# A list scheduler's model of three engines, and the order that it writes for a two-layer transformer kernel

## The chip, the cores and the metric

The kernel runs on one core of a Trainium2 chip. The core has five instruction streams that run side by side and meet at semaphores: TensorE (PE, matrix products), ScalarE (ACT, activation functions), VectorE (DVE, elementwise work), GpSimd (POOL) and SyncE (SP, which issues the transfers). Each of them works through its own list in order. The metric is the device time of one execution in microseconds (us).

## The reference

Two layers are computed one after the other, with the same weights in both: attention with 32 heads of 16 columns, then a dense block with GELU. There are 2048 rows of 512 columns, in bf16.

```python
def _A_ref(x, wqkv, wo):                       # S = 2048, D = 512, H = 32, Dh = 16
    qkv = (x @ wqkv).reshape(B, S, 3, H, Dh).transpose(2, 0, 3, 1, 4)
    q, k, v = qkv[0], qkv[1], qkv[2]
    scores = einsum("bhqd,bhkd->bhqk", q, k) * (Dh ** -0.5)
    p = softmax(scores, axis=-1)
    o = einsum("bhqk,bhkd->bhqd", p, v)
    return o.transpose(0, 2, 1, 3).reshape(B, S, D) @ wo

def _B_ref(x, w1, b1, w2, b2):                 # F = 1792
    h = gelu(einsum("bsd,df->bsf", x, w1) + b1)
    return einsum("bsf,fd->bsd", h, w2) + b2

x = x + _A_ref(layernorm(x), wqkv, wo); x = x + _B_ref(layernorm(x), w1, b1, w2, b2)
x = x + _A_ref(layernorm(x), wqkv, wo); x = x + _B_ref(layernorm(x), w1, b1, w2, b2)
```

## The kernel before

**Cells.** The scores are cut into cells of 128 keys x 512 columns, where the 512 columns are the queries of one head, or of two heads in segments of 256. There are 4,096 cells in the two layers. A pass is one segment of queries and one group of heads; it has four row groups (a = 0 to 3) and 16 key tiles, or a part of them.

**Two ways to an exponential.** TensorE computes the score of a cell into a bank of PSUM (L1137). Most cells go to ScalarE, which takes two or three banks in one instruction (L1466) and writes the probabilities into `pt`. Others go to VectorE: an eviction (`dfirst`, L1283) turns a score into the bits of a bf16 number by a multiply and an add in uint16. Then `dchain` adds a shift to those bits in two further instructions (L1344, L1346), so that four shifted patterns stand in `du`. Each pattern is multiplied with V scaled by a weight of its own (`vc`, copied by GpSimd at L1068), and TensorE sums the four in PSUM. A cell on VectorE therefore asks TensorE for four products with V, one on ScalarE for one. `dchain` works on pairs of cells where it can, or on a single. A column `du`, `dh`, `kt` in the profile's groups names the buffer that holds the patterns. The table `KD` allows VectorE four key tiles of 16 in each layer. What VectorE has not taken when a pass runs out of other cells goes to ScalarE (`next_act`).

**Banks.** PSUM has eight. Banks 0 to 2 and 3 and 4 are two slots (`SLOTS`) that ScalarE empties in turn, bank 5 (`PVB`) gathers the products with V, and banks 6 and 7 serve projections and VectorE's cells.

**The order is written by a simulation.** A generator for each piece of work yields operations (`_Op`) with an engine, a cost in us, and what they read and write. `_Sched.run` keeps a clock for each engine and takes the operation that can start first; among those that could start now on one engine the priority decides. It writes the operations into each engine's list in that order, with the semaphore waits that they need. On the chip the lists run as they stand, so the modelled times have a say only in the order, and in what is decided from the modelled state. These things are decided from it:

- An operation's result is there at its end plus `LATENCY` of its engine (L205, L390). `_cost` (L301) gives the time for which the engine is taken; `SW` = 0.107 is added where TensorE changes between kinds of products.
- A score product may be late by its `slack`, which is the larger of `SLACK` (0.3 us) and the modelled length of the exponential in the other slot less `LATE` (0.7 us). Other TensorE work is taken first only if it ends within that.
- `attach` (L1215) adds up to two VectorE cells to a score operation, if bank 6 or 7 is free within `TOL` = 0.2 us of its start, a `du` buffer is to be had and little other VectorE work waits. `swap` (L1192) turns the third cell of a ScalarE slot into a VectorE cell, if VectorE's modelled clock is no more than `SWAP` = 0.5 us ahead of the start. `solo` places a VectorE cell by itself where ScalarE's modelled clock is far ahead of TensorE's.
- `fill` (L312) puts products without a use into TensorE's modelled gaps, so that it is not idle for long. `free` (L1090) chooses the bank for them. A product into bank 5 has weights of zero and adds nothing to the sum that is gathered there (L1125, `ps<-vc,zero`).

The costs in the code that the change works on are 0.68 us for `dfirst`, 0.08 + 0.14n and 0.08 + 0.28n for the two steps of `dchain` with n cells, 0.065 + 0.4267n for an exponential of n cells, and `MM` = 0.2132 us for a round of four products.

Of the kernel before, what the change touches and what calls it, by code (L numbers as in the profile page):

```python
# [201 lines left out]
        self.done = False  # L202


LATENCY = {"pe": 0.20, "act": 0.103149, "dve": 0.099491, "pool": 0.153328, "sp": 0.1}  # L205


class _Sched:
# [90 lines left out]
        return max(self.end.get(self.P.lastw[k], 0.0) if k in self.P.lastw else 1e9 for k in keys)  # L299

    def _cost(self, op):  # L301
        return op.cost + (SW if op.eng == "pe" and op.mode != self.mode else 0.0)

    def active(self, t):
        while self.stream and self.stream[0][1] < t - WINDOW:
# [6 lines left out]
    def fill(self, start, nxt):  # L312
        while self.filler and self.mode:
# [17 lines left out]
            self.clock["pe"] = now + into + MM + cold  # L331
            self.end[ev] = self.clock["pe"] + LATENCY["pe"]

    def run(self):
        while True:
# [53 lines left out]
            self.clock[e] = start + cost  # L389
            self.end[ev] = start + cost + op.tail + LATENCY[e]  # L390


SW = 0.107
# [108 lines left out]
class _Plan:  # L502
# [587 lines left out]
    def free(self, now, ahead):  # L1090
        P = self.P
        best = (None, 1e9)
        src = self.source()
        for b in (6, 7, 0, 1, 2, 3, 4, 5) if src else ():
            k = "B.%d" % b
            if k in ahead or b in self.hold or k in P.lastw and not P.reads.get(k) and P.lastw[k] not in self.s.fills:
                continue
            t = max([0.0] + [self.s.end.get(ev, 0.0) + FOLD for ev in P.deps(src, [k]) if ev[0] != "pe"])
            if max(t, now) < max(best[1], now):
                best = (b, t)  # L1100
        k = "B.%d" % PVB
        if best[1] > now and self.pvopen and "VC.0.0" in P.lastw and k not in ahead:
            best = (PVB, 0.0)
        return best
# [65 lines left out]
    def take(self, c, free):  # L1170
        self.scored += 1
        self.left[c[0]] -= 1
        if self.left[c[0]] == 0:
            free.append(self.s.tokens[("qp", c[0])])

    def join(self, op, d, b, extra, free):
        pools = self.s.pools
        if self.open is None:
            self.open = {"du": pools["du"].pop(0), "cells": [], "full": False}
        pair = self.open  # L1180
        pair["cells"].append(d)
        extra.append((d, b, pair, len(pair["cells"]) - 1))
        if len(pair["cells"]) == self.cap[pair["du"]]:
            self.open = None
        f, r = self.score(d, self.s.tokens[("qp", d[0])], b)
        op.fns.append(f)
        op.reads += r
        op.writes.append("B.%d" % b)
        self.take(d, free)
        self.nd += 1  # L1190
# [431 lines left out]
```

## Time and profile before

| what | value |
|---|---|
| median of three runs | 1588.72 us (1586.61, 1589.74, 1588.72) |
| span of the profiled execution, first to last instruction | 1584.3 us |
| the profiled execution's own total | not recorded; the median lies 4.4 us above its span |
| busy: TensorE, VectorE, ScalarE | 1432.2, 1355.7, 1545.8 us |
| score products (L1137) | 4,096 |
| VectorE evictions of scores (L1283) | 716 + 92 + 81 = 889 |
| mean granted TensorE clock | 0.998 |
| share of the time in which the DMA engines moved data (q1) | 21.2% |

A group's line gives the line of the kernel, the engine, the operation, output and input by the program's names with their shapes, the count, then busy time and mean duration of one, then the idle time before them and what ended it. A recorded duration goes from an instruction's start to its end; where the next one starts before that end, the engine's time for one is shorter than the duration, and busy time counts an overlap once. The chain that ended last is followed back from the last instruction through what released each one.

### The profile page before, as it was taken

How to read it: one execution, taken by the hardware profiler on the slowest of the kernel's cores; microseconds unless marked ns; L12 is line 12 of the kernel's file. 1: busy time of each engine (PE TensorE's matmuls, PEld its weight loads, DVE VectorE, ACT ScalarE, POOL GpSimd, SP SyncE). 2: the span in 40 equal slices, each digit the busy share in tenths (PEclk: the TensorE clock that was granted, in tenths of full speed). 3: DMA queues.
4: the chain of work that ended last, by engine and by line, in shares of the span. 5: the costliest groups of instructions: out<-in, count | busy, mean ns of one | idle time of the engine just before them, and what ended most of it. 6: DMA issues, size and time to landing. Idle time of an engine off the chain costs nothing.

```text
span 1584.3 us, 43090 instructions
## 1 busy us (share of the span) xinstructions
PE 1432.2 (90%) x18795; PEld 447.9 (28%) x18795; DVE 1355.7 (86%) x2558; ACT 1545.8 (98%) x1392; POOL 200.9 (13%) x250
## 2 busy tenths in 40 slices
PE   8998889999999898998989989888898889889988
PEld 3222222222222222322222222222222222333344
DVE  5689999779998889989799789999789978988894
ACT  7999999999999999999999999999999999999995
POOL 5200011010110201002110020122002000010000
PEclk9999999999999999999999999999999999999999
DMA  5100001341014211152111521001251006213420
GB/s 141 22 1 2 1 16 34 95 126 43 22 48 135 80 41 28 42 149 66 35 28 48 159 50 35 1 14 28 84 151 43 26 9 174 82 36 101 142 82 29
DMA packets 141768, 96.90 MB, mean 61 GB/s; under 512 B 36877, under 2 KB 141582, under 8 KB 141582
## 3 DMA queue, kind: packets, MB, share of 16 engines
q1 hardware_dynamic: 141582, 94.14, 21.2%
q8 instruction: 150, 2.46, 0.6%
q14 instruction: 36, 0.29, 0.1%
HBM read 84.41 MB, written 2.10 MB: 55 GB/s over the span
## 4 chain that ended last, share of the span: by engine, by line
ACT 65%; PE 30%; DVE 2%; POOL 1%; DMA 1%; issue 1%; SPq 0%; POOLq 0%; ACTq 0%
ACT pt L1466 58%; PE ps L512 12%; PE ps L1137 9%; PE ps L1527 9%; ACT g L893 2%; ACT v L1466 1%; ACT kt L1466 1%; ACT q L1466 1%; DVE du L1283 1%; ACT L893 1%; PE ps L1125 1%; DMA xf<-xln 1%; DVE du L1346 0%; ACT L1466 0%; DVE du L1344 0%
## 5 line engine op out<-in xcount | busy, mean ns | idle before, releaser
L1466 ACT ACTIVATE pt<-ps 128x1536 bf16<-128x1536 f32 (+1 forms) x1264 | 1387.1, 1259 | 10.5 <-PE ps L1137 6.4
L1137 PE MATMUL ps<-qp,kt 32*128 32x512 bf16 x4096 | 534.7, 384 | 129.9 <-ACT pt L1466 91.5
L1283 DVE TENSOR_SCALAR du<-ps 128x512 uint16<-128x512 f32 x716 | 484.5, 686 | 92.7 <-PE ps L1137 85.9
L1527 PE MATMUL ps<-pt,v 128*17 128x512 bf16 (+1 forms) x3386 | 444.9, 359 | 3.2 <-DVE v L739 1.1
L1137 PEld LDWEIGHTS ps<-qp,kt 32*128 32x128 bf16 x4096 | 141.2, 91 | 677.1 <-ACT pt L1466 286.1
L1527 PE MATMUL ps<-du,vc 128*17 128x512 bf16 (+1 forms) x2403 | 326.6, 359 | 1.3 <-DVE du L1344 0.6
L1346 DVE TENSOR_SCALAR du<-du 128x2048 uint16<-128x2048 uint16 (+1 forms) x361 | 246.7, 686 | 2.2
L1085 POOL TENSOR_SCALAR qp<-q,mask 128x512 bf16<-128x512 bf16 (+1 forms) x91 | 66.9, 735 | 1005.5 <-PE ps L1137 996.4
L512 PE MATMUL ps<-xf,wr 128*32 128x512 bf16 (+1 forms) x2400 | 171.2, 369 | 3.0 <-DMA xf<-xln 1.6
L1344 DVE TENSOR_SCALAR du<-du 128x1024 uint16<-128x1024 uint16 (+1 forms) x361 | 152.6, 433 | 2.2
L1527 PE MATMUL ps<-du,v 128*17 128x512 bf16 (+1 forms) x801 | 148.3, 360 | 0.8 <-DVE du L1346 0.5
L1527 PEld LDWEIGHTS ps<-pt,v 128*17 128x17 bf16 x3386 | 114.4, 88 | 114.8 <-issue 76.6
L512 PE MATMUL ps<-wr,g 128*32 128x512 bf16 x1600 | 123.2, 386 | 3.9 <-ACT g L893 3.2
L1527 PEld LDWEIGHTS ps<-du,vc 128*17 128x17 bf16 x2403 | 91.0, 89 | 65.4 <-issue 30.2
L872 DVE TENSOR_SCALAR g<-ps,hb1t 128x512 bf16<-128x512 f32 (+1 forms) x112 | 79.9, 713 | 15.3 <-PE ps L512 13.9
L1527 PE MATMUL ps<-dh,vc 128*17 128x512 bf16 (+1 forms) x309 | 86.4, 357 | 0.0
L1283 DVE TENSOR_SCALAR dh<-ps 128x512 uint16<-128x512 f32 x92 | 63.0, 685 | 9.3 <-PE ps L1137 7.9
L512 PEld LDWEIGHTS ps<-xf,wr 128*32 128x32 bf16 x2400 | 52.5, 95 | 61.9 <-issue 33.6
L1283 DVE TENSOR_SCALAR kt<-ps 128x512 uint16<-128x512 f32 x81 | 55.5, 685 | 14.9 <-PE ps L1137 13.9
L602 POOL TENSOR_SCALAR xln<-x,rstd,nmr 128x512 bf16<-128x512 bf16 x58 | 56.3, 973 | 30.9 <-DMA xf<-xln 21.6
L1125 PE MATMUL ps<-vc 128*32 128x512 bf16 x520 | 54.7, 384 | 0.0
L754 POOL TENSOR_TENSOR ott<-xt,rc 128x256 bf16<-128x256 f32 x42 | 33.3, 792 | 164.3 <-DVE rc L746 158.8
(93 smaller groups left out, 1184.5 us busy)
## 6 DMA issues: line engine op xcount, KB each, us to landing
wr<-in_B_w_dram SPq DMA_DIRECT2D x256, 256.0 KB, 2.8
wr<-in_A_wqkv_dram SPq DMA_DIRECT2D x24, 256.0 KB, 2.9
wr<-in_A_wo_dram SPq DMA_DIRECT2D x18, 256.0 KB, 2.9
out_dram<-x SPq DMA_DIRECT2D x16, 128.0 KB, 2.6
g<-in_A_wqkv_dram SPq DMA_DIRECT2D x3, 512.0 KB, 6.0
x<-in_A_x_dram SPq DMA_DIRECT2D x3, 512.0 KB, 8.8
q<-in_B_w_dram SPq DMA_DIRECT2D x3, 512.0 KB, 5.5
kt<-in_B_w_dram SPq DMA_DIRECT2D x4, 256.0 KB, 3.3
```

Of the source, the lines that this page charges most:

```text
L512: return [lambda e, a=a: e.matmul(out[32 * a:32 * a + 32, :], lhsT=lhsT[:, 32 * a:32 * a + 32], rhs=rhs, start=start, stop=stop, tile_posi ...
L602: yield _Op(eng, cost, lambda e: e.tensor_scalar(T["XLN"][:, x, :], T["X"][:, t, :], T["RSTD"][:, t:t + 1], T["NMR"][:, t:t + 1], op0=ALU. ...
L872: yield _Op("dve", 0.21 + n / 966, lambda e, fc=fc, pb=pb: e.tensor_scalar(T["G"][:, fc, q], pb, T["HB1T"][:, fc:fc + 1], None, op0=ALU.ad ...
L893: lambda e, g=g: e.activation(out=g, in_=g, func=ACT.Gelu_apprx_tanh), reads=gk, writes=gk, prio=2)
L1085: yield _Op("pool", 0.1 + 0.6 * w / 512, lambda e, s=s, q=q, i=i, t=t, w=w: e.tensor_scalar(T["QP"][:, s, w * i:w * i + w], q, T["MASK"][: ...
L1125: fns.append(lambda e, o=o, w=w, a=a, m=m: e.matmul(o, lhsT=w, rhs=rhs, start=start, stop=start, tile_position=(0, m * a)))
L1137: return (lambda e: e.matmul(o, lhsT=lhsT, rhs=rhs, start=True, stop=True, tile_position=(32 * a, 0)), ["K%d.%d.%d" % (l, gb, kt // 4), "Q ...
L1283: yield _Op("dve", 0.68, lambda e: e.tensor_scalar(u, self.bank(b), E_SCALE, E_BIAS, op0=ALU.mult, op1=ALU.add), reads=["B.%d" % b], write ...
L1344: yield _Op("dve", 0.08 + 0.14 * n, lambda e: e.tensor_scalar(U[:, 1, 0:n, :], U[:, 0, 0:n, :], SHIFT, None, op0=ALU.add), reads=key[0], w ...
L1346: yield _Op("dve", 0.08 + 0.28 * n, lambda e: e.tensor_scalar(U[:, 2:4, 0:n, :], U[:, 0:2, 0:n, :], 2 * SHIFT, None, op0=ALU.add), reads=k ...
L1466: yield _Op("act", 0.065 + 0.4267 * n, lambda e, src=src, dst=dst: e.activation(out=dst, in_=src, func=ACT.Exp, scale=0.25), reads=["B.%d" ...
L1527: op.fns.append(lambda e, o=o, lhsT=q[0][0][m], rhs=q[0][1][:, n * m:n * m + n], a=a, st=st, sp=sp: e.matmul(o, lhsT=lhsT, rhs=rhs, start= ...
```

## The change

The latencies of TensorE, ScalarE and VectorE in the model are raised. A VectorE operation takes its engine for 0.083 us less than its cost, and for no less than 0.07 us. A TensorE operation of kind "P" (products with V, projections) takes 2% longer. And bank 5 is no longer in the list from which `free` takes a filler's bank first; it is still taken when no other is free and its sum is open. No operation's own code is changed: which cells go to which engine, and the order in every list, follow from the simulation run anew.

```diff
-LATENCY = {"pe": 0.20, "act": 0.103149, "dve": 0.099491, "pool": 0.153328, "sp": 0.1}
+LATENCY = {"pe": 0.219, "act": 0.21, "dve": 0.139, "pool": 0.153328, "sp": 0.1}
+OVERLAP = 0.083
+ROUND = 1.02
...
     def _cost(self, op):
-        return op.cost + (SW if op.eng == "pe" and op.mode != self.mode else 0.0)
+        if op.eng == "dve":
+            return max(op.cost - OVERLAP, 0.07)
+        if op.eng == "pe":
+            return op.cost * (ROUND if op.mode == "P" else 1.0) + (SW if op.mode != self.mode else 0.0)
+        return op.cost
...
-        for b in (6, 7, 0, 1, 2, 3, 4, 5) if src else ():
+        for b in (6, 7, 0, 1, 2, 3, 4) if src else ():
```

## The prediction

> **What bounds the kernel now.** I read the page's busy shares first, then the chain that ended last, then the groups kept apart by shape, the table of waits, and at last one short stretch in order of time. The first view asks which engine has no room:
>
> ```profile
> PE 1432.2 (90%) x18795; PEld 447.9 (28%) x18795; DVE 1355.7 (86%) x2558; ACT 1545.8 (98%) x1392; POOL 200.9 (13%) x250
> ACT 65%; PE 30%; DVE 2%; POOL 1%; DMA 1%; issue 1%; SPq 0%; POOLq 0%; ACTq 0%
> ```
>
> ScalarE (ACT) is full, and the chain runs through it or through TensorE (PE) for 95% of the span. VectorE (DVE) is on it for 2%, so a faster VectorE helps only by taking work from ScalarE. The stretches say where room is:
>
> ```profile
> 0.00:100.00 100.00, 95.30 (x1186) 29.43 (x1186) 64.25 (x132) 90.41 (x92) 33.56 (x55) 1.00 0.25 65
> 100.00:200.00 100.00, 82.83 (x940) 22.65 (x938) 93.45 (x178) 99.74 (x90) 9.73 (x12) 1.00 0.01 2
> 300.00:400.00 100.00, 92.84 (x1167) 27.29 (x1169) 82.10 (x151) 99.63 (x91) 10.16 (x12) 1.00 0.34 96
> 700.00:800.00 100.00, 92.04 (x1138) 26.01 (x1138) 82.54 (x154) 99.75 (x95) 17.32 (x20) 1.00 0.22 62
> ```
>
> The columns are length, then busy PE, weight load, DVE, ACT, POOL with counts. In the three later ones ScalarE is above 99%, while VectorE stands idle for 6 us of 100 in the first stretch after the opening and for 18 in the others shown.
>
> Now the times that the scheduler's model is compared with, by group (count, then busy us, mean ns of one, idle before):
>
> ```profile
> L1466 ACT ACTIVATE pt<-ps 128x1024 bf16<-128x1024 f32 x771 | 806.9, 1092 | 3.0 <-PE ps L1137 2.1
> L1466 ACT ACTIVATE pt<-ps 128x1536 bf16<-128x1536 f32 x493 | 750.0, 1521 | 7.4 <-PE ps L1137 4.3 <-PE ps L1527 1.5
> L1283 DVE TENSOR_SCALAR du<-ps 128x512 uint16<-128x512 f32 x716 | 484.5, 686 | 92.7 <-PE ps L1137 85.9
> L1344 DVE TENSOR_SCALAR du<-du 128x1024 uint16<-128x1024 uint16 x355 | 151.2, 436 | 2.2
> L1346 DVE TENSOR_SCALAR du<-du 128x2048 uint16<-128x2048 uint16 x355 | 244.3, 691 | 2.2
> ```
>
> The table of waits (us in total, times, longest) has the two that matter between the engines:
>
> ```profile
> PE ps L1137 <- ACT pt L1466: 91.5, 239, 1.0
> DVE du L1283 <- PE ps L1137: 85.9, 188, 2.9
> ```
>
> And the stretch in order of time, VectorE's lines alone:
>
> ```profile
> 801.37 0.28 DVE L1344 TENSOR_SCALAR dh<-dh 128x512 uint16<-128x512 uint16 x1
> 801.57 0.42 DVE L1344 TENSOR_SCALAR du<-du 128x1024 uint16<-128x1024 uint16 x1
> 801.91 0.42 DVE L1346 TENSOR_SCALAR dh<-dh 128x1024 uint16<-128x1024 uint16 x1
> 802.24 1.10 DVE L1346 TENSOR_SCALAR du<-du 128x2048 uint16<-128x2048 uint16 x1
> ```
>
> In the last fence the columns are start and duration: each instruction starts 0.08 to 0.09 us before the one ahead of it has ended. Over the whole trace 1,717 of 2,558 VectorE instructions start so.
>
> **The constants against these rows.** For an exponential of three cells the old model has its result at 0.065 + 3 x 0.4267 + 0.103 = 1.448 us after its start; the row says 1.521. For two cells it is 1.021 against 1.092. With 0.21 it becomes 1.555 and 1.128, 0.034 to 0.036 behind the recorded ends. That explains the first wait shown: the old order puts a score product 0.07 us too early behind an exponential, and TensorE, which works in order, stands for 91.5 us. For VectorE the old model takes 0.68 for an eviction (L1283); the trace starts the next one 0.60 later, and 0.68 - 0.083 = 0.597. TensorE's 0.213 + 0.219 = 0.432 lies behind a recorded 0.384.
>
> One family is over-corrected. The two shift-and-add steps of a pair cost 0.36 and 0.64 in the code, so 0.277 and 0.557 in the new model; in the fence the first takes 0.34 to its successor, and back to back the second takes 0.60. Singles become 0.137 and 0.277 against 0.20 and 0.33. With 394 pairs and 101 singles (groups L1344, L1346) the new model is short by 394 x (0.063 + 0.043) + 101 x (0.063 + 0.056) = 54 us of VectorE time, where the old one was long by about 25.
>
> A page of the Trainium skill speaks against the overlap: "VectorE: DVE Perf Modes", section "The DRAIN you can't avoid", has the next Vector instruction wait until the pipe of the one before is empty. By that rule alone the sum would hold no extra cells, and 2,558 x 0.083 = 212 us of planned VectorE time would be missing on the chip. The last fence and the count above it show the opposite for two thirds of the instructions, and the measurement decides.
>
> **The change, part by part.** (1) VectorE's planned time falls by at most 2,558 x 0.083 = 212 us. What uses it are `swap` and `attach`, which hand a score cell to VectorE when its planned queue, a bank and a pattern buffer are free soon enough. VectorE now takes 716 + 92 + 81 = 889 of 4,096 cells (the L1283 groups); the code allows 4 of 16 key tiles, 1,024. Of the 135 missing, about 33 belong to the first 100 us, where 17 of 200 cells went to VectorE because the scaled copies of V come late; 102 are in reach. In 100 to 200 us it took 72 of 290, the full quarter, with 6.5 us idle, so the quarter can be carried where little else lies on it. In 300 to 400 us and 700 to 800 us it took 56, with 18 us idle. A cell costs 0.60 + (0.34 + 0.60)/2 = 1.07 us. The thirteen stretches of 100 us from 200 to 1500 are 87.8% busy on the mean; brought to the 93.45% of the full one they give 13 x 5.65 = 73 us, or 69 cells. Ends: 20 cells if banks and buffers hold as now, 100 if all in reach move. I take 60, a little under the 69, since a bank must be free at the right moment too. On ScalarE a cell is worth 1521 - 1092 = 429 ns: 60 x 0.429 = 25.7 us off a path that ScalarE sets. 20 cells give 8.6, 100 give 42.9.
>
> (2) Each moved cell asks for four column products instead of one. Four make a round of about 0.22 us (rounds start 0.22 apart at L1527), so 0.16 us of TensorE a cell, 10 us for 60. TensorE carries 30% of the chain: 3 us are charged, 0 to 10 the bounds. The rest lies in the 91.5 us of waits at L1137.
>
> (3) The 54 us that VectorE's chains are planned short: VectorE's 228 us of idle time cover most. Without that cover a late VectorE instruction keeps a bank, a score product waits for it, and behind it on TensorE all P·V rounds and projections. Bounds 0 and 54; a fifth of the span (100 to 300 and 1000 to 1100 us) is over 93% busy and has little cover, so I take 54 x 300/1584 = 10.
>
> (4) Later ScalarE and TensorE results move score products back by about 0.1 us in the order and put P·V rounds where TensorE waited. By start-to-start times, what follows a two-cell exponential comes 37 us late in total over its 0.903 us, 28 of these in 82 gaps of over 0.2 us that stand behind P·V or projection work. A truer plan can win back some 20; but the allowance of 0.3 us for a late score is unchanged, and with 0.21 + 0.107 + 0.213 + 0.219 = 0.749 of 0.918 us used, a score at its limit leaves ScalarE 0.13 us short. Bounds -20 and +15; taken as 0.
>
> (5) TensorE's rounds 2% longer in the plan, bank 5 out of the list for fillers, other places for DMA issues on SP and for GpSimd's masks: 0. Fillers (1,048 products at L1125) go only where TensorE would stand; if the 528 into bank 5 went without replacement, the granted clock of 0.998 could fall, and 2% of TensorE's 30% of the chain would be 9 us. Weight loads land in 2.8 us with a DMA share of 0.2, far ahead of use. Opening and tail (the last 26 us have no exponential) can shift by 5 either way.
>
> Sum: the profiled span of 1584.3 - 25.7 + 3 + 10 + 0 = 1571.6; the median of the runs lies 4.4 above that span (the profiled execution's own total is not given), so **1576.0**. With the 13 us of costs in proportion to the cells, 20 cells give 1588.7 - 8.6 + 4.3 = 1584.4, and 100 cells give 1588.7 - 42.9 + 21.7 = 1567.5, or 1552 if 15 of the 20 us in (4) come too: this case's own range is 1552 to 1584.
>
> **Rivals.** A: the score ring runs late. Place: L1137 behind a two-cell exponential. There are 792 of them (x771 and the smaller groups); if half of the scores that follow sit at the 0.3 us limit, 396 x 0.13 = 51 us of gaps stand where 37 are now, and P·V work, now free to fill, makes one score in four later by another 0.1, 792/4 x 0.1 = 20 us. With 20 cells moved and their 4.3 of costs: 1588.7 + 34 - 8.6 + 4.3 = 1618 with all of it, 1601 with half. It decides once the gaps grow by more than the cells save, 8.6 us for 20 of them and 25.7 for 60. For it: 82 gaps exist already, and allowance and margins were left. Against: gaps over 0.2 us come of a plan that had results early, which is mended.
>
> B: VectorE becomes the pacing engine. If 40 of the 54 us reach the path, 1588.7 - 25.7 + 3 + 40 = 1606. It decides from 25.7 - 3 = 22.7 us. Against it: 14% idle VectorE.
>
> C: no more cells, since pattern buffers are freed by TensorE, not by VectorE. Then only (4) and noise in the order remain: 1588 +- 4. Against it: the 85.9 us in which L1283 waited for a score.
>
> **How the numbers follow.** A change of 0.2% (3.2 us) is about what can be told from none here. Forecast 0.56, of which 0.55 faster and 0.01 same; A 0.20 and B 0.12, of which 0.30 slower and 0.02 same; C 0.12, a third to each side. That makes faster 0.59, same 0.07, slower 0.34. The range takes the forecast's lower bound, 1552, and reaches up to B's 1606, past the middle of A; left out are the upper part of A and B, and below it more cells than 100 or all of the gaps.
>
> **What would show it.** Right: L1283 above 930 products, three- and two-cell exponentials holding fewer than 3,170 cells, VectorE's share up, the wait of L1137 for ScalarE well under 91.5 us. A: start-to-start excess behind two-cell exponentials above 50 us. B: L1137 waiting for L1283 above 40 us (10.1 now) with VectorE over 95% busy. C: L1283 within 15 of 889. A longer tail or a clock under 0.98 would be none of these, and the prediction wrong in its cause.

## The result, and the profile after

The changed kernel takes 1606.7 us (median of four runs, 1606.6 to 1608.9), the kernel before on the same chip 1587.9 us. The ratio is 1.0129, with a 95% interval of 1.0108 to 1.0150: slower by about 20 us where 1576 was forecast. The profiled span grew from 1584.3 to 1604.9 us.

Lines of before are shown above; these answer to them. Line numbers are 6 higher after the change (L1137 is L1143, L1283 is L1289, L1466 is L1472). First the busy shares and the chain that ended last, from the page of after:

```profile
PE 1427.3 (89%) x18923; PEld 438.2 (27%) x18923; DVE 1401.6 (87%) x2695; ACT 1532.4 (95%) x1389; POOL 204.7 (13%) x250
DVE 50%; PE 30%; ACT 18%; issue 1%; POOL 0%; DMA 0%; DVEq 0%
```

ScalarE has less to do and is a smaller share of a longer span. VectorE, 2% of the chain before, is half of it now, although its busy share rose by one point only. The share is an average; the stretches show where it is full (length, then busy PE, weight load, DVE, ACT, POOL, then the granted clock, the DMA share and GB/s). Three further stretches of before come first, then those of after:

```profile
200.00:300.00 100.00, 92.32 (x1083) 26.46 (x1080) 93.47 (x177) 98.30 (x90) 12.67 (x13) 1.00 0.11 30
1000.00:1100.00 100.00, 82.74 (x915) 23.21 (x911) 94.24 (x187) 98.24 (x88) 22.74 (x29) 1.00 0.05 12
1200.00:1300.00 100.00, 87.74 (x1073) 25.49 (x1075) 87.63 (x163) 99.76 (x85) 12.34 (x14) 1.00 0.10 25
```

```profile
100.00:200.00 100.00, 81.06 (x966) 21.87 (x956) 99.48 (x194) 96.29 (x87) 9.72 (x12) 1.00 0.01 2
200.00:300.00 100.00, 89.37 (x1088) 24.07 (x1084) 97.35 (x189) 95.83 (x89) 12.86 (x13) 1.00 0.12 30
300.00:400.00 100.00, 92.88 (x1191) 26.82 (x1194) 86.47 (x166) 98.48 (x91) 11.54 (x12) 1.00 0.33 94
1200.00:1300.00 100.00, 87.33 (x1090) 24.26 (x1084) 98.83 (x193) 94.89 (x88) 13.10 (x13) 1.00 0.11 28
```

From 100 to 300 and from 1200 to 1300 us VectorE has hardly any idle time left, and ScalarE, at 99.7% from 100 to 200 us before, is at 96.3%. The table of waits names the path from the one to the other (us in total, times, longest), two lines of before first:

```profile
PE ps L1137 <- DVE du L1283: 10.1, 18, 1.0
ACT pt L1466 <- PE ps L1137: 6.4, 14, 1.8
```

```profile
PEld ps L1143 <- DVE du L1289: 162.7, 288, 1.8
PE ps L1143 <- ACT pt L1472: 65.6, 155, 1.5
DVE du L1289 <- PE ps L1143: 61.2, 81, 4.7
ACT pt L1472 <- PE ps L1143: 37.7, 99, 1.4
PE ps L1143 <- DVE du L1289: 31.2, 73, 1.5
```

The first line of after is the weight loads that stand ahead of the score products; they wait for the same evictions. The score products themselves wait for VectorE's evictions (31.2 us, 10.1 before; with the buffers `dh` and `kt` 42.3, 14.1 before), and ScalarE waits for the score products: 37.7 us, 6.4 before. VectorE in its turn waits less for scores, 61.2 us for 85.9.

The groups kept apart by shape give the cells:

```profile
L1472 ACT ACTIVATE pt<-ps 128x1024 bf16<-128x1024 f32 x818 | 827.6, 1057 | 20.0 <-PE ps L1143 17.3
L1472 ACT ACTIVATE pt<-ps 128x1536 bf16<-128x1536 f32 x430 | 639.0, 1486 | 23.2 <-PE ps L1143 20.4
L1289 DVE TENSOR_SCALAR du<-ps 128x512 uint16<-128x512 f32 x763 | 510.0, 683 | 63.1 <-PE ps L1143 61.2
```

With the smaller groups VectorE evicts 763 + 100 + 87 = 950 cells, 61 more than before, and ScalarE's 844 exponentials of two cells and 486 of three hold 3,146.

**The books.** An exponential is followed by the next after 0.903 us (two cells) or 1.330 us (three) where nothing is late. What the start-to-start times hold above that I call gaps. Before: 37.1 us behind two cells and 3.7 behind three, 40.8 in all. After: 76.5 + 14.0 = 90.5. So gaps +49.7; 61 cells fewer at 1.330 - 0.903 = 0.427 us are -26.0; the tail behind the last exponential is 26.5 us for 29.2, -2.7. The sum is +21.0, the span grew by 20.6. The gain came as forecast, and the gaps took it twice over. The question is where 50 us of gaps come from. All gaps below are read in the same way, each from one profiled execution; executions of one kernel differ by some us (those of before from 1582.4 to 1591.9), so a difference of a few us between two gaps tells nothing.

### The profile page after: what moved, and what is told of

Same layout as the page of the kernel before. It is cut to its first block, busy times and chain, and to the rows that moved or that the text cites. A ratio compares the mean times of both kernels' runs of the same rounds, so it can differ in the third digit from the quotient of the medians.

```text
span 1604.9 us, 43512 instructions
## 1 busy us (share of the span) xinstructions
PE 1427.3 (89%) x18923; PEld 438.2 (27%) x18923; DVE 1401.6 (87%) x2695; ACT 1532.4 (95%) x1389; POOL 204.7 (13%) x250
## 4 chain that ended last, share of the span: by engine, by line
DVE 50%; PE 30%; ACT 18%; issue 1%; POOL 0%; DMA 0%; DVEq 0%
DVE du L1289 18%; ACT pt L1472 12%; PE ps L518 12%; PE ps L1143 9%; PE ps L1533 9%; DVE du L1352 8%; DVE du L1350 5%; ACT g L899 3%; DVE dh L1289 2%; DVE g L878 2%; DVE kt L1289 2%; DVE stats L587 2%; DVE dh L1352 1%; DVE xt L749 1%; DVE kt L1352 1%
## 5 line engine op out<-in xcount | busy, mean ns | idle before, releaser
L1472 ACT ACTIVATE pt<-ps 128x1024 bf16<-128x1024 f32 (+1 forms) x1248 | 1358.1, 1205 | 43.3 <-PE ps L1143 37.7
L1143 PE MATMUL ps<-qp,kt 32*128 32x512 bf16 x4096 | 531.6, 386 | 127.4 <-ACT pt L1472 65.6
L1289 DVE TENSOR_SCALAR du<-ps 128x512 uint16<-128x512 f32 x763 | 510.0, 683 | 63.1 <-PE ps L1143 61.2
L1533 PE MATMUL ps<-pt,v 128*17 128x512 bf16 (+1 forms) x3276 | 423.0, 361 | 6.3 <-DVE du L1352 2.4
L1143 PEld LDWEIGHTS ps<-qp,kt 32*128 32x128 bf16 x4096 | 138.3, 91 | 665.3 <-ACT pt L1472 217.9
L1352 DVE TENSOR_SCALAR du<-du 128x2048 uint16<-128x2048 uint16 (+1 forms) x388 | 265.1, 688 | 3.6
L518 PE MATMUL ps<-xf,wr 128*32 128x512 bf16 (+1 forms) x2400 | 164.3, 368 | 5.2 <-DVE g L878 4.0
L1350 DVE TENSOR_SCALAR du<-du 128x1024 uint16<-128x1024 uint16 (+1 forms) x388 | 164.4, 432 | 4.5
L1533 PEld LDWEIGHTS ps<-pt,v 128*17 128x17 bf16 x3276 | 109.3, 89 | 122.0 <-issue 77.3
L1533 PE MATMUL ps<-dh,vc 128*17 128x512 bf16 (+1 forms) x336 | 95.3, 359 | 0.2 <-DVE kt L1352 0.2
L878 DVE TENSOR_SCALAR g<-ps,hb1t 128x512 bf16<-128x512 f32 (+1 forms) x112 | 79.4, 709 | 10.3 <-PE ps L518 10.3
L1289 DVE TENSOR_SCALAR dh<-ps 128x512 uint16<-128x512 f32 x100 | 68.3, 683 | 10.4 <-PE ps L1143 10.2
L1289 DVE TENSOR_SCALAR kt<-ps 128x512 uint16<-128x512 f32 x87 | 59.3, 682 | 10.5 <-PE ps L1143 9.7
L1533 PE MATMUL ps<-kt,vc 128*17 128x512 bf16 (+1 forms) x330 | 58.9, 338 | 0.9 <-DVE kt L1352 0.6
```

Source lines behind the costliest of these rows:

```text
L518: return [lambda e, a=a: e.matmul(out[32 * a:32 * a + 32, :], lhsT=lhsT[:, 32 * a:32 * a + 32], rhs=rhs, start=start, stop=stop, tile_posi ...
L878: yield _Op("dve", 0.21 + n / 966, lambda e, fc=fc, pb=pb: e.tensor_scalar(T["G"][:, fc, q], pb, T["HB1T"][:, fc:fc + 1], None, op0=ALU.ad ...
L1143: return (lambda e: e.matmul(o, lhsT=lhsT, rhs=rhs, start=True, stop=True, tile_position=(32 * a, 0)), ["K%d.%d.%d" % (l, gb, kt // 4), "Q ...
L1289: yield _Op("dve", 0.68, lambda e: e.tensor_scalar(u, self.bank(b), E_SCALE, E_BIAS, op0=ALU.mult, op1=ALU.add), reads=["B.%d" % b], write ...
L1350: yield _Op("dve", 0.08 + 0.14 * n, lambda e: e.tensor_scalar(U[:, 1, 0:n, :], U[:, 0, 0:n, :], SHIFT, None, op0=ALU.add), reads=key[0], w ...
L1352: yield _Op("dve", 0.08 + 0.28 * n, lambda e: e.tensor_scalar(U[:, 2:4, 0:n, :], U[:, 0:2, 0:n, :], 2 * SHIFT, None, op0=ALU.add), reads=k ...
```

## The experiments

Theory B (VectorE is over-filled because its shift-and-add steps are planned too short) is the first suspect, A (late scores in ScalarE's ring) its rival. Each run was timed beside the kernel before on the same chip; ratios are to that, with 95% intervals.

**e1_chain: the two steps planned at their true length.**

```diff
-        yield _Op("dve", 0.08 + 0.14 * n, lambda e: e.tensor_scalar(U[:, 1, 0:n, :], ...
+        yield _Op("dve", 0.146 + 0.137 * n, lambda e: e.tensor_scalar(U[:, 1, 0:n, :], ...
-        yield _Op("dve", 0.08 + 0.28 * n, lambda e: e.tensor_scalar(U[:, 2:4, 0:n, :], ...
+        yield _Op("dve", 0.149 + 0.267 * n, lambda e: e.tensor_scalar(U[:, 2:4, 0:n, :], ...
```

> The changed kernel, with the costs of VectorE's two shift-and-add steps raised so that, less the 0.083 us, they are what the trace shows from start to start: 0.20 and 0.337 us for the first step (one cell, a pair), 0.333 and 0.60 us for the second. B (VectorE paces, since these steps are planned too short): the waits of L1143 for L1289 fall from 31 to about 10 us, VectorE is no longer above 97% busy from 100 to 300 us, and the time falls to 1570 to 1588 us, with about 945 cells on VectorE. A (scores come late in ScalarE's ring): nothing in the ring is changed, so 1600 us or more, with gaps behind two-cell exponentials still near 76 us.

1588.1 us, ratio 1.0017 (1.0007 to 1.0027), against 1.0129 for the changed kernel: 1.1%, or 18 us, from the costs of two steps. 946 cells stay on VectorE and gaps fall from 90.5 to 70.9 us. The time lies 0.1 us past the upper end of B's range and 12 us below A's. Two of B's signs failed, though. The stretches and the wait of e1_chain:

```profile
100.00:200.00 100.00, 83.93 (x924) 22.52 (x920) 98.81 (x194) 97.88 (x88) 9.87 (x12) 0.98 0.01 2
200.00:300.00 100.00, 89.98 (x1094) 24.21 (x1092) 98.35 (x190) 96.98 (x93) 15.85 (x13) 1.00 0.10 28
```

```profile
PE ps L1143 <- DVE du L1289: 27.5, 66, 1.3
```

VectorE is still over 98% busy there, and score products still wait for it. Over-filling is a part, and 30 us of gaps more than before are left.

**e4_short: the changed kernel's own order, with a faster VectorE.** Both steps work on fewer columns, so that they are about 0.05 us shorter on the chip: for a pair 0.28 and 0.56 us from start to start, where the plan has 0.277 and 0.557.

```diff
-e.tensor_scalar(U[:, 1, 0:n, :], U[:, 0, 0:n, :], SHIFT, ...
+e.tensor_scalar(U[:, 1, 0:n, 0:404], U[:, 0, 0:n, 0:404], SHIFT, ...
-e.tensor_scalar(U[:, 2:4, 0:n, :], U[:, 0:2, 0:n, :], 2 * SHIFT, ...
+e.tensor_scalar(U[:, 2:4, 0:n, 0:470], U[:, 0:2, 0:n, 0:470], 2 * SHIFT, ...
```

> The order of the changed kernel, unchanged, but VectorE's two steps work on fewer columns (404 and 470 of 512, after the first use of each buffer), so that on the chip they are about as short as the plan has them; the last columns of three patterns are stale, the rest is computed as before. B: VectorE keeps up with the plan, and the same order takes 1562 to 1580 us. A: VectorE's durations do not matter, 1603 to 1608 us.

1581.2 us, ratio 0.9971 (0.9957 to 0.9985). No instruction changes its place, and 1.6%, 25 us, is gone; gaps fall to 68.3. Just past B's range, far from A's. The chain of waits of the changed kernel shows what was shortened, here in a stretch where VectorE runs without a pause (start, us, what):

```profile
141.65 0.60 DVE du L1289
142.25 0.34 DVE du L1350
142.59 0.60 DVE du L1289
143.19 0.60 DVE du L1352
```

The eviction takes the 0.60 us that the new model plans (0.597). The steps take 0.34 and 0.60 where it plans 0.277 and 0.557.

**c4_short_before: the control to it.** The same cut in the order of before.

> The control to e4_short: the kernel before, its order unchanged, with VectorE's two steps on 404 and 470 of 512 columns (the last columns of three patterns are stale). If VectorE paces only where it is over-filled, the shorter steps are worth little here: 1582 to 1588 us. If any order gains from them as much as the changed one did (25 us), about 1563 us, and e4_short proves nothing about the plan.

1586.4 us, ratio 0.9993 (0.9983 to 1.0003): nothing, though VectorE is busy 35 us less. Its chain reads:

```profile
ACT 68%; PE 29%; DVE 2%; issue 0%; POOL 0%; DMA 0%; ACTq 0%
```

So the 25 us of e4_short are no gift that any order gets from a shorter VectorE. Of these two orders the changed one alone was paced by it.

**e3_overlap: VectorE's overlap alone.** The changed kernel with `LATENCY` of TensorE and ScalarE as before and `ROUND = 1.0`.

> The changed kernel with the old latencies of TensorE and ScalarE (0.20 and 0.103) and without the 2% on rounds: VectorE's overlap alone, with its own latency of 0.139 and bank 5 out. B: VectorE is over-filled as in the changed kernel, 1598 to 1612 us, waits of L1143 for VectorE above 25 us. A: with the old ring the moved cells are a gain, 1565 to 1582 us.

1600.5 us, ratio 1.0092 (1.0077 to 1.0107), 941 cells, gaps 80.6. The time is in B's range, and L1143 waits 29.3 us for L1289, as B said. With the old ring, then, there is a loss too; but this is also a new order, and what that alone can cost is seen in the next runs. The pair with e6_chain_oldlat below tells more.

**e2_latency: the latencies alone.** The kernel before with one line changed.

```diff
-LATENCY = {"pe": 0.20, "act": 0.103149, "dve": 0.099491, ...
+LATENCY = {"pe": 0.219, "act": 0.21, "dve": 0.099491, ...
```

> The kernel before with the new latencies of TensorE and ScalarE alone (0.219 and 0.21). B: VectorE's plan is as loose as before (L1283 waits for scores for some 80 us), so no large loss, 1582 to 1596 us. A: the late scores alone make the loss, 1600 to 1612 us, with more than 60 us of gaps behind two-cell exponentials.

1603.6 us, ratio 1.0114 (1.0099 to 1.0129), gaps 64.3, 904 cells. B had this one wrong: VectorE is no fuller than before, and 18 us are lost. A's time is met, its sign nearly: 58.1 us behind two-cell exponentials, for more than 60. Either A is right too, or something else is. The waits of e2_latency:

```profile
PE ps L1137 <- ACT pt L1466: 93.8, 232, 1.7
ACT pt L1466 <- PE ps L1137: 18.3, 40, 1.1
```

The wait of the score products for ScalarE, 91.5 us before, has not fallen with the later latencies; ScalarE's wait for score products has grown from 6.4.

**c1_early, c2_round, c3_round98: constants that should not matter, or move the wrong way.** The kernel before with ScalarE's latency at 0.05 us; with rounds of kind "P" 2% longer; with rounds 2% shorter. Each is one constant in `LATENCY` or `_cost`. They test a further theory, D: the kernel's other constants were fitted to the one order that the old model writes, and any other order loses.

> A control: the kernel before with ScalarE's latency in the model moved the other way, from 0.103 to 0.05 us, which no trace supports. A (late latencies leave gaps in the ring): a result that is planned earlier cannot leave more planned gaps, 1578 to 1590 us. New rival D (the constants were fitted to the order that the old model writes, and any other order loses about 1%): 1594 to 1604 us.

> The kernel before with TensorE's rounds 2% longer in the plan and nothing else. A and B: neither VectorE nor the ring's latencies are touched, so 1582 to 1592 us. D: another order is enough, 1594 to 1606 us.

> The mirror of c2_round: the kernel before with TensorE's rounds 2% shorter in the plan instead of longer, which no trace supports. D (any order but the fitted one loses about 1%): 1595 to 1608 us, though the constant moves the other way. If a longer round as such made the loss in c2_round: 1575 to 1590 us.

1603.1 us (ratio 1.0108, 1.0088 to 1.0127), 1603.2 us (1.0107, 1.0084 to 1.0129) and 1610.8 us (1.0144, 1.0120 to 1.0169). D is met in the first two, and the third is 3 us slower still than its range: the latency earlier or later, the rounds longer or shorter, each costs 1.1 to 1.4%. A, which had 1578 to 1590 us for c1_early, missed. VectorE takes 889, 882 and 879 cells, so it is not fuller. The books of c1_early: gaps 52.8 (+12.0), a tail of 34.1 us (+4.9), the span +17.5. Those of c2_round: gaps 52.8 (+12.0), seven cells fewer on VectorE (+3.0), a tail of 32.3 (+3.1), the span +18.9. The losses sit in a few places. In c2_round one is from 1000 to 1100 us, where layer 2 finishes the last key tiles of its first two segments and ScalarE was busy for 98.24 us before. Its stretch in c2_round (columns as above):

```profile
1000.00:1100.00 100.00, 80.65 (x853) 22.46 (x850) 90.79 (x180) 91.41 (x82) 20.69 (x25) 0.95 0.03 8
```

ScalarE is down to 91.41; the changed kernel has 92.05 there, and a faster VectorE brings that to 94.12 only (e4_short). Four other orders from the rules of the kernel before, e2_latency among them, are thus 17 to 23 us slower. That its other constants (priorities, paces, allowances) fit the one order that its model writes is what D reads in this; it is not shown.

**e6_chain_oldlat: true for VectorE, and the old ring.** The steps of e1_chain, with `"pe": 0.20, "act": 0.103149` and `ROUND = 1.0`.

> The changed kernel with VectorE's two steps at their true start-to-start times and with TensorE's and ScalarE's old latencies and no 2% on rounds: what is true of VectorE, and the old ring. If over-filling VectorE and the later latencies each cost about 15 us on their own, this takes neither: 1566 to 1578 us, faster than both kernels, with about 948 cells on VectorE and gaps behind two-cell exponentials under 45 us. If VectorE cannot carry 948 cells at all, 1585 us or more.

1574.4 us, ratio 0.9932 (0.9907 to 0.9957): faster than both kernels, with 948 cells. From e3_overlap it differs in the costs of the two steps alone, and these are worth 1.6% or 25 us (gaps 80.6 to 58.2), as much as in e4_short. The gaps were guessed too small: 58.2 in all, 50.2 behind two cells. The books against before: gaps +17.4, 59 cells -25.2, tail -2.5, together -10.3; the span is 1573.7 for 1584.3. VectorE is 89% busy and still a third of the chain:

```profile
DVE 36%; PE 34%; ACT 28%; issue 1%; POOL 1%; DMA 0%; ACTq 0%
```

and the score products' wait for it is down from 31.2 us:

```profile
PE ps L1143 <- DVE du L1289: 18.0, 40, 0.9
```

**e11_short_best: is VectorE still what paces there?** e6_chain_oldlat with the cut of e4_short.

> The order of e6_chain_oldlat, unchanged, with VectorE's two steps cut in the same way (stale last columns). VectorE is 89% busy there with 948 cells. If it is still among what paces: 1558 to 1568 us. If the cells fit once the steps are planned in full: 1571 to 1575 us.

1572.3 us, ratio 0.9892 (0.9871 to 0.9913). Against e6_chain_oldlat's 0.9932 that is 0.4%, with intervals that overlap; its own runs moved by 2 us. 948 cells fit once the steps are planned in full: shortening them is worth 25 us in the changed order and about 2 to 6 here. It was not the number of cells that VectorE could not carry.

**e9_round and e10_lat: what e1_chain has more than e6_chain_oldlat, piece by piece.** e6_chain_oldlat with `ROUND = 1.02`, and with the latencies 0.219 and 0.21.

> e6_chain_oldlat with the 2% on TensorE's rounds put back. If the 2% costs here what it cost in c2_round: 1584 to 1592 us. If the loss in c2_round belonged to the fitted order of the kernel before alone: 1570 to 1580 us.

> e6_chain_oldlat with the new latencies of TensorE and ScalarE put back, still without the 2%. A (the ring leaves gaps once its latencies are true and the allowance stays): 1582 to 1592 us. If the latencies cost nothing where the order is not the fitted one: 1570 to 1580 us.

1583.2 us (ratio 0.9980, 0.9967 to 0.9992; 929 cells, gaps 58.4) and 1587.5 us (0.9995, 0.9983 to 1.0008; 955 cells, gaps 73.8). The first lies between the two ranges given for it, just short of the upper one; the second is in A's. The 2% costs 0.5% and comes with 19 cells less on VectorE, which are worth 8 us; the latencies cost 0.6% in gaps, 15.6 us of them.

**e7_allowance and e8_chain_allow: the allowance cut with the latencies.** `SLACK = 0.15`, `LATE = 0.75` on e2_latency; `SLACK = 0.17`, `LATE = 0.75` on e1_chain.

> The kernel before with the new latencies (0.219 and 0.21, as in e2_latency) and the allowance for late scores cut by what the latencies grew: SLACK 0.15 and LATE 0.75 in place of 0.3 and 0.7. A: the ring's gaps shrink again, 1582 to 1594 us, gaps over 0.2 us below 30 us in all. D: 1598 to 1606 us, as in e2_latency.

> e1_chain (true VectorE steps, new latencies, 2% on rounds) with the allowance cut to SLACK 0.17 and LATE 0.75. A: gaps behind two-cell exponentials fall by 10 us or more from 57, and the time to 1574 to 1582 us. If the allowance does not matter: 1585 to 1592 us as in e1_chain.

1590.7 us (ratio 1.0020, 1.0008 to 1.0033; gaps 55.3, for 64.3 in e2_latency) and 1583.5 us (0.9971, 0.9962 to 0.9980; gaps 64.1, for 70.9 in e1_chain). Both improve, by 0.9% and 0.5%, the way that A says, and the first lies in A's range. But the gaps over 0.2 us behind two cells in e7_allowance are 41.2 us, not under 30, all gaps behind two cells in e8_chain_allow fell by 2.4 us where 10 were expected and its time lies between the two ranges, and both steps are of the size that a new order moves. A is supported, not shown. D missed in e7_allowance, where it had 1598 to 1606 us: this is a fifth order from the rules of the kernel before, and it costs 3 us.

## Why the prediction was wrong

**The constants against the trace** were read rightly. The corrected pieces hold up: the eviction runs at the planned 0.60, and the two steps are over-corrected as computed. Their old costs, 0.36 and 0.64, were nearly start-to-start times already (0.34 and 0.60), so taking 0.083 off counted the overlap twice.

**(1) The cells** came out as 61 for the 60 forecast, worth 26.0 us for 25.7. All the signs that the prediction named for its being right came too: 950 evictions, 3,146 cells on ScalarE, VectorE's share up, the wait of L1143 for ScalarE down to 65.6 us. They tested the gain and none of the costs. A's sign, over 50 us behind two-cell exponentials, came as well (76.5); B's, over 40 us of waits for L1289, only with all three buffers (42.3).

**(3) The steps planned too short** is the term that failed. It was put at 10 us of 54; undone in the plan it is 18 us (e1_chain), undone on the chip in the same order 25 us (e4_short). The error is in the cover. Term (1) sold part of the 228 us in which VectorE was idle to new cells, while term (3) still counted them as room for the steps' 54 us and took as full only the 300 us that were above 93% before. Had it taken the fourteen stretches that term (1) filled, its rule would have charged 54 x 1400/1584 = 48 us, too much. And idle time on the mean of 100 us is no cover: e4_short runs the same list, so its profiled execution can be set against that of the changed kernel exponential by exponential. Of the 21.9 us by which it is shorter, 7.6 are gained from 100 to 300 and 1200 to 1300 us, where VectorE was full, and 15.8 from 300 to 1200 us, where it was 79 to 93% busy; the rest loses 1.5. Rival B had this mechanism, with 40 us and 1606; its time was met by luck, by a sum of two things of which it knew one.

**(4) The later latencies**, taken as 0 between -20 and +15: e10_lat measures 0.6%, about 10 us, and e2_latency 18 us, more than the upper bound. The gaps over 0.2 us behind two cells, 28 us before, of which a truer plan was to win back some 20, grew to 44.7 in e2_latency. Nor does a result that the model has 0.07 us too early explain the 91.5 us in which L1137 waits for ScalarE: with the later latencies alone they are 93.8. That this wait would fall, to 65.6 in the changed kernel, came true for another reason. It goes with VectorE's plan, being 74.0 in e6_chain_oldlat with the old latencies and 73.6 in e10_lat with the new.

**What no step of the sum held** is D. The forecast treated the order as the old one with edits, and noise in it as 4 to 5 us either way. Four other orders from the rules of the kernel before cost 17 to 23 us each, whichever way a constant moved; a fifth, e7_allowance, costs 3. Of the changed kernel's 50 us of gaps about 20 go with over-filling (90.5 to 70.9 in e1_chain, to 68.3 in e4_short), 13 more with the latencies and the 2% (58.2 in e6_chain_oldlat), and 17 are left there, with no cause shown. How much of the 13 is A, true of any order, and how much is the lot that one order draws, stays open: each setting writes one order only. The same holds for e6_chain_oldlat, which is a faster kernel by measurement, and one draw. What VectorE's longer latency and moving bank 5 out of the list do alone was not tried.

A part of these losses goes with TensorE's clock, which is at half for some 3 to 10 us at a time in the traces: for 6.8 us in all in the profiled execution of before, 23.9 in the changed kernel's, 20.5 in c1_early's and 37.5 in c2_round's. The gaps that end in these times or within 2 us behind them come to 1.5, 9.6, 7.0 and 11.0 us; in c2_round that is most of the 12.0 that it has more than before. Whether the orders leave TensorE idle and the clock follows, or the clock comes first, no run separates. The result itself is not a matter of the clock: the runs of the changed kernel had 0.991 to 0.993, and those of the kernel before with as much took 1586.3 to 1590.2 us.

**(2), (5).** TensorE's extra products (7,824 with V for 7,626) brought no visible loss: its idle time ahead of L1143 is 127.4 us for 129.9. The mean clock granted was 0.993 for 0.998. Two small readings were off: the last exponential ends 29.2 us before the end, not 26, and the runs on record lie 1.8 us above their spans; if that holds for the profiled execution of before, 2.6 of the 4.4 us added at the end of the sum are only its being shorter than the median.

**The rule set against the overlap** (the Trainium skill, "VectorE: DVE Perf Modes", "The DRAIN you can't avoid": the next Vector instruction waits for the pipe to empty, though the same paragraph lets one that is not held start earlier) does not hold as a general one in the runs either, and the exception is the common case: evictions follow each other after 0.60 us for a recorded 0.683, and the plan that counts on it with true steps, e6_chain_oldlat, places 59 more cells and is faster.

## What to carry to other kernels

Before a duration in a scheduler's model is corrected, find out whether each number in it is a duration or a start-to-start time; a uniform correction to a mixed table makes some entries wrong, and those on the engine that the plan will now fill are the ones that cost. Idle time can be spent once: what a plan sells to new work is no longer cover for its errors, and an engine that is idle for a tenth of the time on average can still be late where it matters. And where hand-set constants steer a list scheduler, measure a few meaningless perturbations first, since they tell what a new order costs by itself, here 1.1 to 1.4% in three of them, before a cause is read into a difference.

## What the runs showed that was not expected

A VectorE add on uint16 from SBUF to SBUF follows its predecessor after 0.20, 0.34 and 0.60 us for 512, 1,024 and 2,048 columns, with recorded durations of about 0.28, 0.42 and 0.68 (medians of those that overlap): the 0.083 us of overlap are the same for these sizes, and so weigh most on the short ones.

A true latency did not write the better order. With the old latencies, which have ScalarE's results 0.07 us too early and TensorE's 0.02 us sooner than the new ones, the order is faster in both pairs of runs (before against e2_latency, e6_chain_oldlat against e10_lat). TensorE waits at score products for ScalarE as long in the one as in the other (91.5 and 93.8 us, 74.0 and 73.6). What grows with the later latencies is ScalarE's own wait for score products, 6.4 to 18.3 us and 15.5 to 25.2. Why is not shown. Earlier still, at 0.05 us in c1_early, was no better.
